# A new opening for a fused attention and feed-forward kernel: loads in the order k, q, v, the first block's attention in half blocks, and three PSUM banks shared by both layers

## The chip, the cores and the metric

The kernel runs on one core of a Trainium2 chip. The core has four compute engines that run side by side, each through its own list of instructions in order: TensorE (PE, matrix multiplication, with its weight loads shown apart as PEld), VectorE (DVE), ScalarE (ACT) and GpSimd (POOL). POOL also issues the loads of this kernel, SyncE (SP) the stores. The metric is the device time of one execution in microseconds; lower is better. Of the kernel before, three executions were timed: 582.8, 583.45 and 583.76 us, median 583.45.

## The reference

```python
def _attn_ref(q, k, v, E, F):            # q, k, v: 8 batches, 8 heads, 1024 tokens, 64 wide
    k_proj = np.einsum('ks,bhsd->bhkd', E, k)      # E, F: 64 x 1024
    v_proj = np.einsum('ks,bhsd->bhkd', F, v)
    scale = 1.0 / np.sqrt(q.shape[-1])
    scores = scale * np.matmul(q, k_proj.transpose(0, 1, 3, 2))
    scores = scores - np.max(scores, axis=-1, keepdims=True)
    attn = np.exp(scores)
    attn = attn / (np.sum(attn, axis=-1, keepdims=True) + 1e-09)
    return np.matmul(attn, v_proj)

def _moe_ref(x, w_in, w_out):            # x: 8192 x 512, w_in: 512 x 2048, w_out: 2048 x 512
    h = x @ w_in
    g = h * (1.0 / (1.0 + np.exp(-1.702 * h)))
    return (g @ w_out).astype(np.float32)
```

The attention output of all heads, 512 wide, is the x of the feed-forward layer. All inputs and the output are float32 in memory; the loads convert to bf16 on the way, and the multiplications take bf16 and add up in float32.

## The kernel before

**Tiling.** The 8 batches are cut into 16 blocks of 512 tokens, two to a batch. For a batch, TensorE projects k and v with E and F (`proj`, L112: eight matmuls for k and eight for v, which stand in alternation and write the two halves of one PSUM tile), transposes the projected k (L127) and q (`q_tr`, L141: four groups of eight transposes). For a block `h` and a pair of heads `p` there are one scores matmul with an exponential on ACT (`scores`, L155 and L158), and in `outp` one matmul with ones for the softmax's denominator (`d_ps`, L168), one for its numerator (`n_ps`, L170), a reciprocal on DVE (L172) and a product on DVE (L173) that gives a quarter of `xT`, the block's input to the feed-forward layer.

**Feed-forward layer.** `ffn1(j, fc)`, sixteen times a block: four matmuls of 128 x 512 (L184), then the gelu on ACT (L186). `ffn2(j, n, half)`, eight times a block: eight matmuls (L197), and after each second one a copy of the finished 128 x 512 output tile on ACT (L200). The exponential and the gelu need different tables on ACT; a table is loaded by ACT_TABLE_LOAD.

**Order.** It is written out by hand. A block has 24 slots: 16 after the `ffn1` calls and 8 after the `ffn2` calls. The table `fill` holds what is put into a slot. With `j0` the first block of batch `b`, block `j0 - 2` takes the projection of `b` (two of the eight steps in each of the slots 1 to 4), its output in slot 5, the q transposes in slots 8, 10, 12 and 14; the scores of block `h` stand in block `h - 2`, slots 16, 18, 20 and 22, and its `outp` in block `h - 1`, slots 0, 6, 12 and 17. Batch 0 and the scores of blocks 0 and 1 come before all that, with the four `outp` of block 0.

**PSUM.** Eight banks: two for `h_ps`, two for `o_ps`, two for everything named `s_ps`, one each for `d_ps` and `n_ps`.

**Loads.** All on POOL's queue, in this order: E, F, then of batch 0 k and v in halves by heads (k, v, k, v), q in eight pieces (one for each j, runs of 64 elements), w_in in four pieces, w_out in four, then k, v and q of batch 1. POOL issues at most eight that have not landed: the ninth waits for the first.

Of the kernel before, what the change touches and what calls it, by code (L numbers as in the profile page):

```python
# [17 lines left out]
def kernel(ctx, tc, q, k, v, E, F,  # L18
                                                     moe_w_in, moe_w_out, out):
    nc = tc.nc  # L20
# [46 lines left out]
    def load_kv(b, parts=1):  # L67
        kt[b] = ldpool.tile([P, H, J, D], BF16, name="k_sb")
        vt[b] = ldpool.tile([P, H, J, D], BF16, name="v_sb")
        hs = H // parts  # L70
        for i in range(parts):
            for src, dst in ((k, kt[b]), (v, vt[b])):
                nc.gpsimd.dma_start(  # L73
                    out=dst[:, i * hs:(i + 1) * hs],
                    in_=src[b, i * hs:(i + 1) * hs].rearrange("h (p j) d -> p h j d", p=P))
# [6 lines left out]

    nc.gpsimd.dma_start(out=ef_sb[:, 0, :], in_=E)
# [23 lines left out]
    def proj(b, j):  # L107
        def go():
            if j == 0:
                kvps[b] = ps_s.tile([P, H, D], F32, name="s_ps")  # L110
            for e, src in ((0, kt[b]), (1, vt[b])):
                nc.tensor.matmul(kvps[b][e * KP:(e + 1) * KP], eft[:, e, j, :], src[:, :, j, :],  # L112
                                 start=(j == 0), stop=(j == J - 1))
        return go

    def proj_out(b):
        def go():
            ps = kvps.pop(b)
            k_b = att.tile([KP, H, D], BF16, name="k_b")
            nc.vector.tensor_copy(k_b, ps[:KP])  # L120
            vv = ps[KP:].rearrange("k (p t) d -> k p t d", t=2)
            vbd = vbds[b % 2]
            nc.vector.tensor_copy(vbd[:KP, :, :D], vv[:, :, 0, :])
            nc.vector.tensor_copy(vbd[KP:, :, D:], vv[:, :, 1, :])  # L124
# [8 lines left out]

    def q_tr(b, g):
        def go():
            if g == 0:
                qT[b] = att.tile([P, HP, J, P], BF16, name="qT")
            t_ps = ps_s.tile([P, 2, HP, P], BF16, name="s_ps")
            for jj in range(2):
                for p in range(HP):  # L140
                    nc.tensor.transpose(  # L141
                        t_ps[:, jj, p, :],
                        qt[b][:, 2 * g + jj, 2 * p:2 * p + 2, :].rearrange("s t d -> s (t d)"), ident)
            nc.vector.tensor_copy(qT[b][:, :, 2 * g:2 * g + 2, :],  # L144
                                  t_ps.rearrange("r j p s -> r p j s"))
        return go
# [14 lines left out]
    def outp(h, p):  # L161
        b, c = divmod(h, S // TB)

        def go():
            if p == 0:
                xT[h] = att.tile([P, KC, TB], BF16, name="xT", bufs=3)
            d_ps = ps_n.tile([P, TB], F32, name="d_ps")
            nc.tensor.matmul(d_ps, ones2, expT[h][:, p, :], start=True, stop=True)  # L168
            n_ps = ps_n.tile([P, TB], F32, name="n_ps")
            nc.tensor.matmul(n_ps, vbds[b % 2][:, p, :], expT[h][:, p, :], start=True, stop=True)  # L170
            rden = att.tile([P, TB], F32, name="rden")
            nc.vector.reciprocal(rden, d_ps)  # L172
            nc.vector.tensor_tensor(xT[h][:, p, :], n_ps, rden, op=ALU.mult)  # L173
# [3 lines left out]
    gts, osb = {}, {}  # L177

    def ffn1(j, fc):
        if fc == 0:  # L180
            gts[j] = work.tile([P, FC, TB], BF16, name="gT")
        h_ps = ps_h.tile([P, TB], F32, name="h_ps")
        for kc in range(KC):
            nc.tensor.matmul(h_ps, w_in_sb[:, kc, fc * P:(fc + 1) * P], xT[j][:, kc, :],  # L184
                             start=(kc == 0), stop=(kc == KC - 1))
        nc.scalar.activation(gts[j][:, fc, :], h_ps, AF.Gelu_apprx_sigmoid)  # L186

    o_ps = {}

    def ffn2(j, n, half):  # L190
# [3 lines left out]
        if half == 0:  # L194
            o_ps[0] = ps_o.tile([P, DM], F32, name="o_ps")
# [13 lines left out]
    def at(j, slot, f):  # L209
        fill.setdefault((j, slot), []).append(f)  # L210

    NB2 = S // TB
    for b in range(1, B):
# [9 lines left out]
    for h in range(1, NBLK):  # L223
        for p, slot in enumerate((0, 6, 12, 17)):
            at(h - 1, slot, outp(h, p))


    for j in range(J):
        proj(0, j)()
    proj_out(0)()  # L230
    for g in range(J // 2):
        q_tr(0, g)()
    for h in range(NB2):
        for p in range(HP):
            scores(h, p)()
    for p in range(HP):
        outp(0, p)()
    load_kv(1)
    load_q(1)
# [43 lines left out]
```

## Time and profile before

| | |
|---|---|
| median of three executions | 583.45 us |
| profiled execution, its own time | 582.58 us |
| its span (first to last instruction) | 580.8 us |
| PE busy | 534.1 us, 92% of the span |
| DVE busy | 297.5 us, 51% |
| ACT busy | 264.9 us, 46% |
| POOL busy | 79.1 us, 14% |
| mean granted clock of TensorE | 0.978 |

The profile is one execution. The time of that execution is 1.78 us more than its span. "Granted clock" is the share of TensorE's full clock that it was given; a matmul on a granted clock of 0.50 takes twice as long to stream. A row of a timeline gives the start, the duration, the engine and line, the operation with output and input, and, in square brackets, how long the engine had been idle before it and which engine's or transfer's end released it. DMA traffic in GB/s counts the bytes as they are written, in bf16.

### The profile page before, as it was taken

How to read it: one execution, taken by the hardware profiler on the slowest of the kernel's cores; microseconds unless marked ns; L12 is line 12 of the kernel's file. 1: busy time of each engine (PE TensorE's matmuls, PEld its weight loads, DVE VectorE, ACT ScalarE, POOL GpSimd, SP SyncE). 2: the span in 40 equal slices, each digit the busy share in tenths (PEclk: the TensorE clock that was granted, in tenths of full speed). 3: DMA queues.
4: the chain of work that ended last, by engine and by line, in shares of the span. 5: the costliest groups of instructions: out<-in, count | busy, mean ns of one | idle time of the engine just before them, and what ended most of it. 6: DMA issues, size and time to landing. Idle time of an engine off the chain costs nothing.

```text
span 580.8 us, 6222 instructions
## 1 busy us (share of the span) xinstructions
PE 534.1 (92%) x2621; PEld 241.4 (42%) x2672; DVE 297.5 (51%) x209; ACT 264.9 (46%) x414; POOL 79.1 (14%) x98
## 2 busy tenths in 40 slices
PE   0635999999999999999999999999999999999997
PEld 0301444435444444435444444444444354444443
DVE  1385555547462764628373672737364573546200
ACT  0121446445463545545364545544464554645251
POOL 7533450013100140002300140000000000000000
PEclk9966999999999999999999999999999999999999
DMA  9999999029900691019910493010010101010001
GB/s 141 181 206 190 191 191 149 2 73 165 111 14 1 142 148 73 0 74 149 72 69 1 111 171 82 1 73 1 0 73 1 73 0 73 0 73 1 37 36 73
DMA packets 90379, 46.80 MB, mean 81 GB/s; under 512 B 67312, under 2 KB 87792, under 8 KB 88432
## 3 DMA queue, kind: packets, MB, share of 16 engines
q0 software_dynamic: 87616, 29.63, 45.7%
q1 hardware_dynamic: 2736, 16.78, 7.0%
q8 instruction: 21, 0.34, 0.2%
q14 instruction: 6, 0.05, 0.0%
HBM read 59.24 MB, written 16.78 MB: 131 GB/s over the span
## 4 chain that ended last, share of the span: by engine, by line
PE 85%; DMA 8%; ACT 5%; POOL 1%; issue 1%; ACTq 0%; POOLq 0%
PE o_ps L197 38%; PE h_ps L184 37%; DMA v_sb<-in_v_dram 6%; ACT L186 3%; PE s_ps L112 2%; PE s_ps L141 2%; PE s_ps L155 2%; PE n_ps L170 2%; DMA w_in_sb<-in_moe_w_in_dram 2%; PE d_ps L168 2%; ACT gT L186 1%; PE s_ps L127 0%; POOL k_sb L73 0%; ACT o_sb L200 0%; POOL q_sb L81 0%
## 5 line engine op out<-in xcount | busy, mean ns | idle before, releaser
L172 DVE RECIPROCAL rden<-d_ps 128x512 f32<-128x512 f32 x64 | 214.8, 3356 | 184.3 <-PE d_ps L168 179.7
L184 PE MATMUL h_ps<-xT,w_in_sb 128*128 128x512 bf16 x1000 | 243.9, 383 | 10.0 <-ACT gT L186 6.6
L197 PE MATMUL o_ps<-w_out_sb,gT 128*128 128x512 bf16 x1002 | 233.4, 379 | 1.2
L186 ACT ACTIVATE gT<-h_ps 128x512 bf16<-128x512 f32 x256 | 151.3, 597 | 131.8 <-PE h_ps L184 131.7
L184 PEld LDWEIGHTS <-w_in_sb 128*128 128x128 bf16 x1024 | 97.4, 98 | 130.7 <-issue 25.1
L197 PEld LDWEIGHTS <-gT 128*128 128x128 bf16 x1024 | 100.2, 98 | 120.8
L158 ACT ACTIVATE expT<-s_ps 128x512 bf16<-128x512 f32 x64 | 37.8, 597 | 88.1 <-PE s_ps L155 87.3
L200 ACT COPY o_sb<-o_ps 128x512 f32<-128x512 f32 x64 | 37.4, 585 | 86.0 <-PE o_ps L197 83.1
L81 POOL DMA_DIRECT2D q_sb<-in_q_dram x64 | 56.1, 902 | 79.9 <-PE s_ps L141 39.9
L173 DVE TENSOR_TENSOR xT<-n_ps,rden 128x512 bf16<-128x512 f32 x64 | 44.3, 692 | 6.7
L73 POOL DMA_DIRECT2D k_sb<-in_k_dram x9 | 7.7, 860 | 183.9 <-PE s_ps L112 181.3
L168 PE MATMUL d_ps<-expT,ones 128*128 128x512 bf16 x59 | 23.2, 394 | 8.6 <-DVE rden L172 8.6
L112 PE MATMUL s_ps<-k_sb,eft 128*64 128x512 bf16 x64 | 22.2, 437 | 9.0 <-DMA k_sb<-in_k_dram 9.0
L112 PE MATMUL s_ps<-v_sb,eft 128*64 128x512 bf16 x64 | 22.0, 440 | 5.7 <-DMA v_sb<-in_v_dram 5.7
L144 DVE COPY qT<-s_ps 128x1024 bf16<-128x1024 bf16 x32 | 21.3, 683 | 10.9 <-PE s_ps L141 10.9
L170 PE MATMUL n_ps<-expT,vbd 128*128 128x512 bf16 x64 | 25.1, 393 | 0.9 <-DVE xT L173 0.6
L155 PE MATMUL s_ps<-qT,kbd 128*128 128x512 bf16 x64 | 24.3, 380 | 1.4 <-ACT expT L158 0.8
L120 DVE CAST k_b<-s_ps 64x512 bf16<-64x512 f32 x8 | 5.5, 682 | 38.6 <-PE s_ps L112 38.6
L141 PE MATMUL s_ps<-ident,q_sb 128*128 128x128 bf16 x256 | 20.7, 230 | 0.6 <-DVE vbd L124 0.6
L141 PEld LDWEIGHTS <-q_sb 128*128 128x128 bf16 x256 | 18.2, 104 | 7.4 <-issue 0.7
L186 ACT ACT_TABLE_LOAD x15 | 19.2, 1283 | 4.2 <-PE h_ps L184 4.2
L158 ACT ACT_TABLE_LOAD x15 | 19.2, 1283 | 2.4 <-PE s_ps L155 1.4
(29 smaller groups left out, 60.4 us busy)
## 6 DMA issues: line engine op xcount, KB each, us to landing
out_dram<-o_sb SPq DMA_DIRECT2D x15, 1024.0 KB, 3.9
q_sb<-in_q_dram POOLq DMA_DIRECT2D x64, 128.0 KB, 6.0
k_sb<-in_k_dram POOLq DMA_DIRECT2D x7, 1024.0 KB, 10.5
v_sb<-in_v_dram POOLq DMA_DIRECT2D x7, 1024.0 KB, 14.6
w_in_sb<-in_moe_w_in_dram POOLq DMA_DIRECT2D x4, 512.0 KB, 10.7
w_out_sb<-in_moe_w_out_dram POOLq DMA_DIRECT2D x4, 512.0 KB, 17.5
k_sb<-in_k_dram POOLq DMA_DIRECT2D x2, 512.0 KB, 8.9
v_sb<-in_v_dram POOLq DMA_DIRECT2D x2, 512.0 KB, 10.6
```

The lines of the kernel that those rows point to most:

```text
L81: nc.gpsimd.dma_start(out=qt[b][:, j], in_=qv[:, j])
L112: nc.tensor.matmul(kvps[b][e * KP:(e + 1) * KP], eft[:, e, j, :], src[:, :, j, :], start=(j == 0), stop=(j == J - 1))
L141: nc.tensor.transpose(t_ps[:, jj, p, :], qt[b][:, 2 * g + jj, 2 * p:2 * p + 2, :].rearrange("s t d -> s (t d)"), ident)
L155: nc.tensor.matmul(s_ps, kbds[b % 2][:, p, :], qT[b][:, p, c * JB:(c + 1) * JB, :].rearrange("r j s -> r (j s)"), start=True, stop=True)
L158: nc.scalar.activation(expT[h][:, p, :], s_ps, AF.Exp, scale=scale)
L170: nc.tensor.matmul(n_ps, vbds[b % 2][:, p, :], expT[h][:, p, :], start=True, stop=True)
L172: nc.vector.reciprocal(rden, d_ps)
L173: nc.vector.tensor_tensor(xT[h][:, p, :], n_ps, rden, op=ALU.mult)
L184: nc.tensor.matmul(h_ps, w_in_sb[:, kc, fc * P:(fc + 1) * P], xT[j][:, kc, :], start=(kc == 0), stop=(kc == KC - 1))
L186: nc.scalar.activation(gts[j][:, fc, :], h_ps, AF.Gelu_apprx_sigmoid)
L197: nc.tensor.matmul(o_ps[0], gts[j][:, fc, n * P:(n + 1) * P], w_out_sb[:, fc, :], start=(fc == 0), stop=(fc == FC - 1))
L200: nc.scalar.copy(osb[j][:, n, :], o_ps[0])
```

## The change

**Loads.** k and q and v of batch 0 now come in this order, each in two pieces by j (runs of four j, 256 elements, that is 512 bytes as written), q no longer in eight pieces of 64-element runs but in the layout of k and v. Then w_in in eight pieces, w_out in four, and k, q, v of batch 1 right behind. Later batches load in the order k, q, v.

**Opening.** The k projection alone comes first, then the q transposes of block 0's half, the scores of block 0, and the denominators of its first 256 tokens (two pairs of heads to one PSUM tile of 128 x 512); then the second half of the q transposes, with their copies on ACT, the scores of block 1, a gelu table load, and only then the v projection, its casts on ACT, the numerators of the first 256 tokens and the denominators of the second. The transposes of batch 0 take one head at a time (64 of them in place of 32), because of q's new layout.

**Block 0.** Its `ffn1` runs as 16 calls on the first 256 tokens and 16 on the second, and the rest of the attention of blocks 0 and 1 and the work of batch 1 are put into its slots.

**Everywhere.** `h_ps` and `o_ps` share one pool of three banks, `d_ps` gets two and `n_ps` one; `outp` is cut into `den` and `num`; the projection goes in as two groups of four steps (slots 1 and 3); the scores stand in slots 16 to 19, followed by an explicit load of the gelu table in slot 20.

On ACT, in the opening, before (`expT` is the exponentials, `gT` the gelu outputs, each row with its count):

```order
L158 ACT_TABLE_LOAD
L158 ACTIVATE expT<-s_ps 128x512 x8
L186 ACT_TABLE_LOAD
L186 ACTIVATE gT<-h_ps 128x512 x16
L158 ACT_TABLE_LOAD
```

And in the changed kernel (`qT` the transposed q, `vbd` the projected v):

```order
L176 ACT_TABLE_LOAD
L176 ACTIVATE expT<-s_ps 128x512 x4
L163 COPY qT<-s_ps 128x4x256 x2
L176 ACTIVATE expT<-s_ps 128x512 x4
L180 ACT_TABLE_LOAD
L142 CAST vbd_91<-s_ps 64x4x64
L143 CAST vbd_91<-s_ps 64x4x64
L230 ACTIVATE gT<-h_ps 128x256 x32
L242 COPY o_sb<-o_ps 128x512 x4
```

Two qT copies and the two v casts moved to ACT; the gelu table load now stands ahead of the casts, and block 0 has 32 gelus of half the width.

On DVE, in the opening, before:

```order
L120 CAST k_b<-s_ps 64x512
L123 CAST vbd_91<-s_ps 64x4x64
L124 CAST vbd_91<-s_ps 64x4x64
L130 COPY kbd_90<-s_ps 64x4x64
L131 COPY kbd_90<-s_ps 64x4x64
L144 COPY qT<-s_ps 128x4x256 x4
L172 RECIPROCAL rden<-d_ps 128x512
L173 TENSOR_TENSOR xT<-n_ps,rden 128x512
```

And in the changed kernel:

```order
L127 CAST k_b<-s_ps 64x512
L133 COPY kbd_90<-s_ps 64x4x64
L134 COPY kbd_90<-s_ps 64x4x64
L163 COPY qT<-s_ps 128x4x256 x2
L204 RECIPROCAL rden<-d_ps 128x512 x2
L216 TENSOR_TENSOR xT<-n_ps,rden 128x2x256 x2
L204 RECIPROCAL rden<-d_ps 128x512 x2
L216 TENSOR_TENSOR xT<-n_ps,rden 128x2x256 x2
L204 RECIPROCAL rden<-d_ps 128x512 x2
L216 TENSOR_TENSOR xT<-n_ps,rden 128x512
L204 RECIPROCAL rden<-d_ps 128x512
L216 TENSOR_TENSOR xT<-n_ps,rden 128x512
```

Two reciprocals, not four with their products in between, stand ahead of the products on which block 0's first matmuls wait; behind them the reciprocals run ahead of the products by one or two.

On ACT, from one block's gelus to the next block's, in a later block, before:

```order
L186 ACTIVATE gT<-h_ps 128x512 x16
L158 ACT_TABLE_LOAD
L158 ACTIVATE expT<-s_ps 128x512
L200 COPY o_sb<-o_ps 128x512
L158 ACTIVATE expT<-s_ps 128x512
L200 COPY o_sb<-o_ps 128x512
L158 ACTIVATE expT<-s_ps 128x512
L200 COPY o_sb<-o_ps 128x512
L158 ACTIVATE expT<-s_ps 128x512
L200 COPY o_sb<-o_ps 128x512
L186 ACT_TABLE_LOAD
L186 ACTIVATE gT<-h_ps 128x512 x16
```

And in the changed kernel:

```order
L230 ACTIVATE gT<-h_ps 128x512 x16
L176 ACT_TABLE_LOAD
L176 ACTIVATE expT<-s_ps 128x512
L242 COPY o_sb<-o_ps 128x512
L176 ACTIVATE expT<-s_ps 128x512 x2
L242 COPY o_sb<-o_ps 128x512
L176 ACTIVATE expT<-s_ps 128x512
L180 ACT_TABLE_LOAD
L242 COPY o_sb<-o_ps 128x512 x2
L230 ACTIVATE gT<-h_ps 128x512 x16
```

The gelu table load moved from behind the block's last output copy to ahead of the last two; their number is the same.

```diff
-    ps_h = ctx.enter_context(tc.tile_pool(name="ps_h", bufs=2, space=PSUM))
-    ps_o = ctx.enter_context(tc.tile_pool(name="ps_o", bufs=2, space=PSUM))
+    ps_f = ctx.enter_context(tc.tile_pool(name="ps_f", bufs=3, space=PSUM))
     ps_s = ctx.enter_context(tc.tile_pool(name="ps_s", bufs=2, space=PSUM))
+    ps_d = ctx.enter_context(tc.tile_pool(name="ps_d", bufs=2, space=PSUM))
     ps_n = ctx.enter_context(tc.tile_pool(name="ps_n", bufs=1, space=PSUM))
...
+    def load_kv(src, dst, b, name, js=J):
+        dst[b] = ldpool.tile([P, H, J, D], BF16, name=name)
+        for j in range(0, J, js):
+            nc.gpsimd.dma_start(
+                out=dst[b][:, :, j:j + js],
+                in_=src[b].rearrange("h (p j) d -> p h j d", p=P)[:, :, j:j + js])
...
-    load_kv(0, parts=2)
-    load_q(0)
+    load_kv(k, kt, 0, "k_sb", JB)
+    load_kv(q, qt, 0, "q0_sb", JB)
+    load_kv(v, vt, 0, "v_sb", JB)
...
-    for i in range(4):
-        sl = slice(i * DFF // 4, (i + 1) * DFF // 4)
+    for i in range(8):
+        sl = slice(i * DFF // 8, (i + 1) * DFF // 8)
         nc.gpsimd.dma_start(out=w_in_sb[:, :, sl], in_=w_in_v[:, :, sl])
...
+    load(1)
...
+    def v_out(b):
+        def go():
+            vv = kvps.pop((b, 1))[KP:].rearrange("k (p t) d -> k p t d", t=2)
+            vbd = vbds[b % 2]
+            cp = nc.scalar.copy if b == 0 else nc.vector.tensor_copy
+            cp(vbd[:KP, :, :D], vv[:, :, 0, :])
+            cp(vbd[KP:, :, D:], vv[:, :, 1, :])
+        return go
...
+                if b == 0:
+                    for h in range(H):
+                        r = h % 2 * D
+                        nc.tensor.transpose(t_ps[r:r + D, jj, h // 2, :], qt[b][:, h, j, :], ident)
...
+            cp = nc.scalar.copy if b == 0 and g >= 2 else nc.vector.tensor_copy
+            cp(qT[b][:, :, 2 * g:2 * g + 2, :], t_ps.rearrange("r j p s -> r p j s"))
...
+    def gelu_table():
+        nc.scalar.preload_act_table(AF.Gelu_apprx_sigmoid)
+    def unit(h, p0, pn=1, half=None):
+        return (h, slice(p0, p0 + pn),
+                slice(0, TB) if half is None else slice(half * TB // 2, (half + 1) * TB // 2))
+    def over(ps, lhsT, u):
+        h, ps_, ts = u
+        for i, p in enumerate(range(ps_.start, ps_.stop)):
+            nc.tensor.matmul(ps[:, i, :], lhsT(p), expT[h][:, p, ts], start=True, stop=True)
+    def den(*a):
+        u = unit(*a)
+        def go():
+            d_ps = ps_d.tile(shape(u), F32, name="d_ps")
+            over(d_ps, lambda p: ones2, u)
+            rdens[a] = att.tile(shape(u), F32, name="rden", bufs=4)
+            nc.vector.reciprocal(rdens[a], d_ps)
+        return go
+    def num(*a):
...
+            n_ps = ps_n.tile(shape(u), F32, name="n_ps")
+            over(n_ps, lambda p: vbds[h // (S // TB) % 2][:, p, :], u)
+            nc.vector.tensor_tensor(xT[h][:, u[1], u[2]], n_ps, rdens.pop(a), op=ALU.mult)
+        return go
...
+    O = FC
+    proj(0, range(J), (0,))()
+    k_out(0)()
+    for g in (0, 1):
+        q_tr(0, g)()
+    for p in range(HP):
+        scores(0, p)()
+    den(0, 0, 2, 0)()
+    den(0, 2, 2, 0)()
+    for g in (2, 3):
+        q_tr(0, g)()
+    for p in range(HP):
+        scores(1, p)()
+    gelu_table()
+    proj(0, range(J), (1,))()
+    v_out(0)()
+    num(0, 0, 2, 0)()
+    num(0, 2, 2, 0)()
+    den(0, 0, 2, 1)()
+    den(0, 2, 2, 1)()
+    at(0, 9, num(0, 0, 2, 1))
+    at(0, 15, num(0, 2, 2, 1))
+    at(0, 16, den(1, 0), den(1, 1))
+    at(0, 23, num(1, 0))
+    at(0, 28, den(1, 2), num(1, 1))
+    at(0, 32 + 1, den(1, 3), num(1, 2))
+    at(0, 32 + 3, num(1, 3))
+    at(0, 32 + 5, proj(1, range(J), (0,)), k_out(1))
+    at(0, 32 + 6, q_tr(1, 0))
+    at(0, 32 + 7, q_tr(1, 1), *[scores(2, p) for p in range(HP)], gelu_table)
+    at(1, 2, q_tr(1, 2))
+    at(1, 4, q_tr(1, 3))
+    at(1, 5, proj(1, range(J), (1,)), v_out(1))
+    for p, slot in enumerate((6, 11, O, O + 2)):
+        at(1, slot, den(2, p), num(2, p))
...
-        for j in range(J):
-            at(j0 - 2, 1 + j // 2, proj(b, j))
-        at(j0 - 2, 5, proj_out(b))
+        for j in range(0, J, 4):
+            at(j0 - 2, 1 + j // 2, proj(b, range(j, j + 4)))
+        at(j0 - 2, 5, k_out(b), v_out(b))
...
-                at(j0 + c - 2, 16 + 2 * p, scores(j0 + c, p))
+                at(j0 + c - 2, O + p, scores(j0 + c, p))
+            at(j0 + c - 2, O + HP, gelu_table)
```

The slots of block 0 run to 39: 0 to 15 after the first half's `ffn1`, 16 to 31 after the second half's, 32 to 39 after the `ffn2` calls.

More of the change, by code (lines that the diff above doesn't have):

```diff
@@ L159, in scores @@
         return go
-    def outp(h, p):
-        b, c = divmod(h, S // TB)
-        def go():
-            if p == 0:
-                xT[h] = att.tile([P, KC, TB], BF16, name="xT", bufs=3)
[L167 to L173, printed above, removed]
-        return go
@@ L181, in ffn1 @@
+    gts, osb, o_ps = {}, {}, {}
+    def ffn1(j, fc, ts=slice(0, TB)):
+        if j not in gts:
             gts[j] = work.tile([P, FC, TB], BF16, name="gT")
-        h_ps = ps_h.tile([P, TB], F32, name="h_ps")
+        n = ts.stop - ts.start
+        h_ps = ps_f.tile([P, n], F32, name="h_ps", tag="f_ps")
         for kc in range(KC):
-            nc.tensor.matmul(h_ps, w_in_sb[:, kc, fc * P:(fc + 1) * P], xT[j][:, kc, :],
+            nc.tensor.matmul(h_ps, w_in_sb[:, kc, fc * P:(fc + 1) * P], xT[j][:, kc, ts],
@@ L185, in ffn1 @@
                              start=(kc == 0), stop=(kc == KC - 1))
-        nc.scalar.activation(gts[j][:, fc, :], h_ps, AF.Gelu_apprx_sigmoid)
-    o_ps = {}
+        nc.scalar.activation(gts[j][:, fc, ts], h_ps, AF.Gelu_apprx_sigmoid)
     def ffn2(j, n, half):
```

108 lines of the change are left out of this document (49 added, 59 removed).

## The prediction

> **What bounds the kernel now.** I read the page first (shares, groups), then the timeline of the opening, then TensorE's waits behind it.
>
> ```profile
> span 580.8 us, 6222 instructions
> PE 534.1 (92%) x2621; PEld 241.4 (42%) x2672; DVE 297.5 (51%) x209; ACT 264.9 (46%) x414; POOL 79.1 (14%) x98
> L172 DVE RECIPROCAL rden<-d_ps 128x512 f32<-128x512 f32 x64 | 214.8, 3356 | 184.3 <-PE d_ps L168 179.7
> L144 DVE COPY qT<-s_ps 128x1024 bf16<-128x1024 bf16 x32 | 21.3, 683 | 10.9 <-PE s_ps L141 10.9
> L200 ACT COPY o_sb<-o_ps 128x512 f32<-128x512 f32 x64 | 37.4, 585 | 86.0 <-PE o_ps L197 83.1
> L123 DVE CAST vbd<-s_ps 64x256 bf16<-64x256 f32 x8 | 3.4, 427 | 0.3
> ```
>
> TensorE bounds the kernel as a whole. Its idle time lies in the opening, in this timeline (start, duration, engine, line, operation; in brackets the idle time before and its releaser):
>
> ```profile
> 21.05 0.68 DVE L120 CAST k_b<-s_ps 64x512 bf16<-64x512 f32 x1 [14.71 <-PE s_ps L112]
> 21.80 0.39 PE L127 MATMUL s_ps<-ident,k_b 64*128 64x64 bf16 x4 [0.78 <-DVE k_b L120]
> 22.79 3.66 PE L141 MATMUL s_ps<-ident,q_sb 128*128 128x128 bf16 x32 [0.60 <-DVE vbd L124]
> 26.37 0.49 PE L155 MATMUL s_ps<-qT,kbd 128*128 128x512 bf16 x1
> 26.90 4.52 ACT L158 ACTIVATE expT<-s_ps 128x512 bf16<-128x512 f32 x8 [24.88 <-PE s_ps L155]
> 31.04 3.36 DVE L172 RECIPROCAL rden<-d_ps 128x512 f32<-128x512 f32 x1 [3.87 <-PE s_ps L155]
> 34.51 0.69 DVE L173 TENSOR_TENSOR xT<-n_ps,rden 128x512 bf16<-128x512 f32 x1
> 47.43 0.58 PE L184 MATMUL h_ps<-xT,w_in_sb 128*128 128x512 bf16 x1 [2.19 <-DVE xT L173]
> 54.67 0.59 PE L112 MATMUL s_ps<-v_sb,eft 128*64 128x512 bf16 x1 [3.76 <-DMA v_sb<-in_v_dram]
> ```
>
> Four reciprocals in series, each with its product, hold the first `ffn1` until 47.43; then the v of batch 1 stops TensorE until 54.67. From there it hardly stops. What is left are stops at block starts:
>
> ```profile
> PE h_ps L184 <- ACT gT L186: 6.6, 14, 0.7
> 90.35 0.58 ACT o_sb L200
> 90.95 1.28 ACT L186
> 92.24 0.61 ACT gT L186
> 92.24 1.09 ACT L186 ACTIVATE gT<-h_ps 128x512 bf16<-128x512 f32 x2
> 92.89 4.48 PE L184 MATMUL h_ps<-xT,w_in_sb 128*128 128x512 bf16 x20 [0.42 <-ACT gT L186]
> 97.20 0.38 PE L168 MATMUL d_ps<-expT,ones 128*128 128x512 bf16 x1
> 120.95 1.03 PE L184 MATMUL h_ps<-xT,w_in_sb 128*128 128x512 bf16 x4
> 159.19 4.48 PE L184 MATMUL h_ps<-xT,w_in_sb 128*128 128x512 bf16 x20 [0.73 <-ACT gT L186]
> 190.30 1.02 PE L184 MATMUL h_ps<-xT,w_in_sb 128*128 128x512 bf16 x4 [0.18 <-ACT gT L186]
> ```
>
> The last copy of a block is followed by the gelu table load, 1.28 us, and the third group of `ffn1` waits for a PSUM bank. Twenty matmuls from 92.89 to 97.20 give a step of 0.216 us. A matmul's row lasts 0.38, so a gap listed as 0.18 or 0.73 costs 0.16 more: 0.34 and 0.89.
>
> **Part 1: the loads.** The queue's own waits and the windows (width, PE, granted clock, DMA share, GB/s):
>
> ```profile
> 9.94 0.88 POOL L81 DMA_DIRECT2D q_sb<-in_q_dram  x1 [0.79 <-DMA k_sb<-in_k_dram]
> 12.49 0.87 POOL L81 DMA_DIRECT2D q_sb<-in_q_dram  x1 [1.67 <-DMA v_sb<-in_v_dram]
> 10.00:15.00 5.00, 0.07 (x1) 1.00 1.24 205
> 17.00:22.00 5.00, 3.80 (x19) 1.00 2.42 154
> 47.50:50.50 3.00, 3.00 (x7) 0.50 1.24 204
> 51.00:53.50 2.50, 0.00 (x0) 1.00 1.33 202
> 57.20:60.40 3.20, 3.20 (x11) 0.50 2.34 160
> 61.00:64.00 3.00, 3.00 (x19) 1.00 1.25 209
> ```
>
> The first piece of 512 KB is there at 9.9, the next 2.55 later. The new runs of 512 bytes as written lie between those of 1024 (205 GB/s) and q's of 128 (154). I take 200, nearer the first since a run of 512 has a quarter of the starts that q's has: 2.6 us a piece. Then k is complete at 12.5, q at 15.1 and 17.7, v at 20.3 and 22.9, w_in at 33.4, w_out at 43, k of batch 1 at 48. None of the last three is needed before it lands (below), so the load of batch 1 that stopped TensorE until 54.67 no longer does.
>
> **Part 2: the opening, on a half clock.** Second half of the k projection: 12.5 + 4 x 0.43 + 0.2 = 14.4 (0.43 is twice the step above). Cast 0.68 and transposes 0.4: 15.5. The first 32 one-head transposes cost 0.11 each if they run in series (3.66 / 32): 3.5 us; if two heads run side by side in the two column halves, as k and v do in the projection, 1.75. With the last qT copy of 0.68 behind, the scores of block 0 start between 18.2 and 19.9; I take 19. Four exponentials at 0.56 (4.52 / 8) and 0.53 ahead: 21.8. Denominators 0.85, then the second 32 transposes with their two copies on ACT, for which there is no row at 1024 elements: between 0.6 (512 take 0.585) and 1.2, taken 1.0. Scores of block 1 start at 25.4 to 27.0, taken 26.3; their exponentials end at 29.1. The v projection waits for an `s_ps` bank until 28.6 and takes 8 x 0.43 + 0.2: 32.2. The gelu table load, 29.1 to 30.4, is hidden below it, and costs its 1.3 if the projection gets shorter. Two casts on ACT, at most 0.585 each, taken 0.4: 33.1. Two times numerator (0.6) and product (0.69), one after the other since `n_ps` has one bank, with some 0.1 of handover: `ffn1` starts at **36.0**, bounds 34 and 38.5. The two reciprocals ahead, 21.9 to 28.6, are covered by the v chain.
>
> **Part 3: blocks 0 and 1.** TensorE's own work in block 0 at full clock: 128 half matmuls at 0.108 (bounds 0.108 and 0.12) 13.8; `ffn2` 64 x 0.216 = 13.8; numerators and denominators 4 x 0.108 + 8 x 0.216 = 2.2; k projection 1.9; transposes 1.1; scores 0.9. Sum 33.7. Stops: a half clock for 3.4 to 7 us more, worth 2.6 (bounds 1.7 and 3.5). The second half's last product stands one slot ahead of its first matmul: 0.75. In slot 28 the numerator waits for `n_ps`, whose product stands on DVE behind a second reciprocal (den(1,0), den(1,1), then the product: 2 x 3.36 + 0.7 after slot 16, where TensorE has 6.3 of work): 1.7, with the last three `ffn1` and all of `ffn2` queued behind it. The same in slot 35: 0.7. The k projection of batch 1 has its transposes straight behind the cast: 0.95. The scores of block 2 stand right behind the qT copy, 0.95, and share two banks with their exponentials, 1.35. Sum 9.0; block 1 starts at 36.0 + 33.7 + 9.0 = 78.7. Block 1: 27.6 + 0.9 + 1.9 + 1.7 + 0.9 = 33.0. Block 2 starts at 111.7, and not at 120.95: **9.3** gained. Both kernels have done the same work by then. w_out is used from 54, k of batch 1 from 65, v from 85; all have landed.
>
> **Part 4: blocks 2 to 14.** The gelu table now loads during `ffn2`, and a third bank lets `ffn1` run on. Even blocks lose 0.34 today, six times; odd ones and block 14 0.89, seven times: 8.3, all of it gained if nothing else comes last; none if ACT comes last all the same. The projection:
>
> ```profile
> 127.03 1.04 PE L184 MATMUL h_ps<-xT,w_in_sb 128*128 128x512 bf16 x4
> 127.99 0.40 PE L112 MATMUL s_ps<-k_sb,eft 128*64 128x512 bf16 x1
> 128.23 0.38 PE L112 MATMUL s_ps<-k_sb,eft 128*64 128x512 bf16 x1
> 128.55 1.04 PE L184 MATMUL h_ps<-xT,w_in_sb 128*128 128x512 bf16 x4
> ```
>
> Two steps take 0.56 and 0.1 of entry; two groups of four take 2 x (0.56 + 2 x 0.24 + 0.1) = 2.3 in place of 4 x 0.66 = 2.6; six times that is 2.2 gained (nothing, if the entry grows with the group). Scores in adjoining slots, `v_out` behind `k_out` and v loaded last cost nothing: an exponential of 0.6 fits below the 1.73 of a slot (eight matmuls), DVE is half idle, and a load has two blocks of time. **10.5** in all.
>
> **Sum.** 580.8 - 9.3 - 10.5 = 561.0 of span. The profiled execution took 582.58, 1.78 more than its span, and the median lies 0.87 above it: 561.0 + 1.78 + 0.87 = **563.7**.
>
> [...] By the chain above, copy, load (1.28) and gelu follow each other within 0.02 us. [...]
>
> **The rivals.**
> *The clock is full before `ffn1`.* After 3 us of unbroken work (47.5 to 50.5) the windows show a full clock, though TensorE then idles; 57.2 to 60.4 ends alike. The new opening is nearly unbroken from 20.2 to 25.5 if the transposes run in series. Then the v projection halves (1.7), numerators save 0.3 and the 2.6 of block 0 is gone: 563.7 - 4.6 = 559.1. Against it: the transposes from 22.79 still took 0.11 each, right after 3.5 us of projection, and 54.67 to 60.4 stayed at half. [...]
> *Half gelus bind.* If 256 elements cost ACT about as much as 512 (0.6; 0.5 back to back, by the two in the row from 92.24), 32 of them take 16 to 19 us against TensorE's 13.8: 4 more, 568.
> *The boundary gain fails.* The load moves, but ACT is still last with the first gelu: 8.3 lost, 572. Against it: after the early load only one copy of 0.585 stands ahead of that gelu.
> *Slower: short runs starve the weights.* k, q, v and w_in, 5.24 MB, now all come in runs of 512 bytes, and the first half block needs all of w_in. By the forecast that half is through at about 45 (36.0 and some 9 on the partly half clock); 20 us later, no gain is left. From 7.4 on that is a rate of 5240 / 57 = 92 GB/s; at 80 the end is 8 us beyond, near 592. Against it: 128-byte runs reached 154.
>
> **How the numbers follow.** Forecast 0.48, full clock early 0.30, half gelus 0.12, no boundary gain 0.07, starved 0.03. The forecast's own range, from the bounds of 36.0 and of the stops, is 561 to 567. The range given, 556.5 to 570, takes in the second and third case. A difference below 0.2% (1.2 us) could not be told from no change; faster 0.95, same 0.02, slower 0.03.
>
> **What would show it.** Right: `ffn1`'s first row near 36 with product and numerator just ahead; full clock some 5 us later; block 2 near 112; TensorE's waits for gT at later block starts gone; table loads ahead of the last two copies. Wrong: a clock of 1.00 already at 26; `ffn1` waiting for w_in; gT as the releaser all through block 0; a TensorE gap of more than 3 us at slots 28, 35 or 39, or a new wait in each block.

## The result, and the profile after

The changed kernel takes 557.09 us in the median (556.03 to 559.95), the one before 583.44 in the same series: a ratio of 0.9557, with a 95% interval of 0.9519 to 0.9596. The forecast was 563.7, in a range of 556.5 to 570. Three slow executions of the series below are left out of the medians and ratios: 1900.85 us of the kernel without the early table load (in its trace the matmuls of the two layers last 1011 and 1053 ns in the mean, 371 and 379 in the changed kernel, so this kernel was run a second time for a trace), 1702.99 of the reordered kernel, and 600.37 of the kernel before.

The page of the changed kernel, whose profiled execution (559.95 us) was the longest of its four:

```profile
span 558.2 us, 6473 instructions
PE 535.2 (96%) x2776; PEld 252.8 (45%) x2776; DVE 294.8 (53%) x205; ACT 269.0 (48%) x434; POOL 77.3 (14%) x96
L228 PE MATMUL h_ps<-xT,w_in_sb 128*128 128x512 bf16 (+1 forms) x1088 | 241.5, 371 | 0.7 <-DVE xT L216 0.6
```

TensorE is as busy as before (535 us), in a span that is 22.6 us shorter. Ahead of `ffn1` it was idle for 10.0 us in all before, 6.6 of them for gT; now for 0.7, and gT is no releaser.

The timeline of the opening and of blocks 0 and 1:

```profile
12.04 1.87 PE L119 MATMUL s_ps<-k_sb,eft 128*64 128x512 bf16 x4 [0.68 <-DMA k_sb<-in_k_dram]
15.00 1.92 PE L156 MATMUL s_ps<-ident,q_sb 128*64 128x128 bf16 x32
17.71 1.01 PE L173 MATMUL s_ps<-qT,kbd 128*128 128x512 bf16 x2 [0.79 <-DVE qT L163]
22.14 1.93 ACT L163 COPY qT<-s_ps 128x1024 bf16<-128x1024 bf16 x2 [1.46 <-PE s_ps L156]
24.12 0.59 PE L173 MATMUL s_ps<-qT,kbd 128*128 128x512 bf16 x2 [1.19 <-ACT qT L163]
26.24 3.53 PE L119 MATMUL s_ps<-v_sb,eft 128*64 128x512 bf16 x8 [0.20 <-ACT expT L176]
30.63 0.39 PE L192 MATMUL n_ps<-expT,vbd 128*128 128x256 bf16 x2 [0.85 <-ACT vbd L143]
32.45 6.49 PE L228 MATMUL h_ps<-xT,w_in_sb 128*128 128x256 bf16 x40
42.78 0.38 PE L228 MATMUL h_ps<-xT,w_in_sb 128*128 128x256 bf16 x2 [0.56 <-DVE xT L216]
50.58 0.38 PE L192 MATMUL n_ps<-expT,vbd 128*128 128x512 bf16 x1 [1.32 <-DVE xT L216]
59.92 0.38 PE L192 MATMUL n_ps<-expT,vbd 128*128 128x512 bf16 x1 [0.32 <-DVE xT L216]
66.38 0.29 PE L130 MATMUL s_ps<-ident,k_b 64*128 64x64 bf16 x4 [0.78 <-DVE k_b L127]
71.90 0.59 PE L173 MATMUL s_ps<-qT,kbd 128*128 128x512 bf16 x2 [0.78 <-DVE qT L163]
73.25 0.87 PE L173 MATMUL s_ps<-qT,kbd 128*128 128x512 bf16 x2 [0.76 <-ACT expT L176]
73.96 4.44 PE L228 MATMUL h_ps<-xT,w_in_sb 128*128 128x512 bf16 x12
108.79 1.03 PE L228 MATMUL h_ps<-xT,w_in_sb 128*128 128x512 bf16 x4
```

`ffn1` starts at 32.45 and hardly stops; the stops named in the prediction are there, each a little shorter. Block 1 starts at 73.96, block 2 at 108.79. Against 120.95 the opening and blocks 0 and 1 gave 12.2 us; from block 2 to the end it is 449.4 us now and was 459.9, so 10.4 more.

The windows of the same execution (stretch, width, PE busy, granted clock, DMA share, GB/s):

```profile
26.40:29.80 3.40, 3.37 (x8) 0.53 1.45 196
30.00:33.00 3.00, 1.46 (x11) 1.00 1.44 198
33.00:36.40 3.40, 3.40 (x17) 0.50 1.25 207
70.60:74.00 3.40, 1.74 (x14) 1.00 1.66 192
74.00:77.40 3.40, 3.40 (x10) 0.50 1.14 342
77.40:80.00 2.60, 2.60 (x20) 1.00 1.19 216
```

The clock does not rise once and stay. Up to 23 us TensorE is on half speed by the lengths of its rows (two scores matmuls take 1.01 at 17.71 and 0.59 at 24.12), although the windows there read 1.00: in this trace the record shows no half clock ahead of the first fall, and so the mean granted clock of an execution leaves this stretch out. Then the clock is full for the scores at 24, half for the v projection (3.53 us for eight matmuls, 1.91 in the k projection of batch 1 at 63.69), full again, half for the first 3.4 us of `ffn1`, and half once more for the first 3.4 us of block 1. Each of the three falls comes after a stretch in which TensorE was busy for about half of the time (1.48, 1.64 and 1.74 of the 3.4 us before).

### The profile page after: what moved, and what is told of

It reads as the page before. It is cut to its first block, busy times and chain, and to the rows that moved or that the text cites. A ratio compares the mean times of both kernels' runs of the same rounds, so it can differ in the third digit from the quotient of the medians.

```text
span 558.2 us, 6473 instructions
## 1 busy us (share of the span) xinstructions
PE 535.2 (96%) x2776; PEld 252.8 (45%) x2776; DVE 294.8 (53%) x205; ACT 269.0 (48%) x434; POOL 77.3 (14%) x96
## 4 chain that ended last, share of the span: by engine, by line
PE 93%; DVE 2%; ACT 2%; DMA 2%; issue 1%; POOL 0%; POOLq 0%
PE h_ps L228 40%; PE o_ps L239 39%; PE s_ps L119 4%; PE n_ps L192 3%; PE s_ps L173 2%; PE d_ps L192 2%; PE s_ps L159 2%; DMA k_sb<-in_k_dram 2%; DVE rden L204 1%; ACT expT L176 1%; DVE xT L216 1%; PE s_ps L156 1%; PE s_ps L130 0%; ACT qT L163 0%; DVE k_b L127 0%
## 5 line engine op out<-in xcount | busy, mean ns | idle before, releaser
L228 PE MATMUL h_ps<-xT,w_in_sb 128*128 128x512 bf16 (+1 forms) x1088 | 241.5, 371 | 0.7 <-DVE xT L216 0.6
L230 ACT ACTIVATE gT<-h_ps 128x512 bf16<-128x512 f32 (+1 forms) x272 | 155.5, 572 | 120.6 <-PE h_ps L228 119.4
L228 PEld LDWEIGHTS <-w_in_sb 128*128 128x128 bf16 x1088 | 105.3, 99 | 116.4 <-issue 10.6
L78 POOL DMA_DIRECT2D q_sb<-in_q_dram x56 | 49.0, 902 | 79.4 <-PE s_ps L159 59.4
L216 DVE TENSOR_TENSOR xT<-n_ps,rden 128x512 bf16<-128x512 f32 x64 | 44.0, 688 | 12.9 <-PE n_ps L192 7.0
L192 PE MATMUL n_ps<-expT,vbd 128*128 128x512 bf16 (+1 forms) x68 | 24.3, 366 | 3.3 <-DVE xT L216 2.4
L192 PE MATMUL d_ps<-expT,ones 128*128 128x512 bf16 (+1 forms) x68 | 24.4, 374 | 0.0
L119 PE MATMUL s_ps<-k_sb,eft 128*64 128x512 bf16 x64 | 18.3, 415 | 4.3 <-DMA k_sb<-in_k_dram 4.3
L119 PE MATMUL s_ps<-v_sb,eft 128*64 128x512 bf16 x64 | 18.1, 414 | 0.2 <-ACT expT L176 0.2
L159 PE MATMUL s_ps<-ident,q_sb 128*128 128x128 bf16 x224 | 17.1, 219 | 0.0
L119 PEld LDWEIGHTS <-eft 128*64 128x64 bf16 x128 | 8.5, 115 | 18.1 <-issue 14.4
```

The lines of the kernel that those rows point to most:

```text
L78: nc.gpsimd.dma_start(out=qt[b][:, j], in_=qv[:, j])
L119: nc.tensor.matmul(kvps[b, e][e * KP:(e + 1) * KP], eft[:, e, j, :], (kt, vt)[e][b][:, :, j, :], start=(j == 0), stop=(j == J - 1))
L159: nc.tensor.transpose(t_ps[:, jj, p, :], qt[b][:, j, 2 * p:2 * p + 2, :].rearrange("s t d -> s (t d)"), ident)
L192: nc.tensor.matmul(ps[:, i, :], lhsT(p), expT[h][:, p, ts], start=True, stop=True)
L216: nc.vector.tensor_tensor(xT[h][:, u[1], u[2]], n_ps, rdens.pop(a), op=ALU.mult)
L230: nc.scalar.activation(gts[j][:, fc, ts], h_ps, AF.Gelu_apprx_sigmoid)
```

## The experiments

### Which of two edits took the waits at the block starts away

The prediction gave 8.3 us to the early table load and the third bank together. Two kernels take one away or add one alone. First the changed kernel without the early load in blocks 1 to 13:

```diff
-    at(1, O + HP, gelu_table)
-            at(j0 + c - 2, O + HP, gelu_table)
```

> The changed kernel without the explicit gelu table load in blocks 1 to 13, so that the load falls due again at each block's first gelu; three shared banks stay. If the early load is what took the waits at the block starts away (part 4 of the prediction), they come back: 0.34 in even and 0.89 us in odd blocks and block 14, about 8 us in all, and the stretch from the start of block 2 to the end goes from 449.4 to about 457 us. Rival: the third bank alone covers the load. After a block's last matmul ACT needs copy 0.6, a wait of 0.3 for the first group, load 1.28 and gelu 0.6, 2.8 us, while TensorE has three groups of 0.86 and the 0.43 of a denominator and numerator, 3.0: then the stretch stays at 449 to 450 us and the time does not change.

Measured: 558.23 us, ratio to the kernel before 0.9557 (0.953 to 0.9584), the same as with the load. The same kernel, run again:

> The same kernel as the one without the early gelu table load, since the profile of the first was of an execution in which TensorE ran at less than a third of its speed throughout. If the third bank alone covers the load, TensorE shows no wait for gT at any block start and the stretch from block 2 to the end is 449 to 450 us; if not, 457.

Measured: 556.04 and 561.10 us, ratio 0.9603 (0.9561 to 0.9645). The timeline of the execution of 556.04, span 554.3 us: first TensorE's start of block 2, then ACT's table load and TensorE's third and fourth groups:

```profile
104.70 1.03 PE L228 MATMUL h_ps<-xT,w_in_sb 128*128 128x512 bf16 x4
105.81 1.28 ACT L230 ACT_TABLE_LOAD   x1 [0.32 <-PE h_ps L228]
107.94 1.90 PE L228 MATMUL h_ps<-xT,w_in_sb 128*128 128x512 bf16 x8
```

The table load is back where it was, and no row of TensorE from here on waits for gT. From 104.70 to the end it is 449.6 us. So in the changed kernel the early load is worth nothing: the third bank covers it.

Next the kernel before with the early load alone:

```diff
+    def gelu_table():
+        nc.scalar.preload_act_table(AF.Gelu_apprx_sigmoid)
...
+            at(j0 + c - 2, 16 + 2 * HP - 2, gelu_table)
```

> The kernel before, and in it only the early gelu table load, behind the last exponential of a block in slot 22, so ahead of the block's last output copy. PSUM pools as before (two banks for each layer). If the early load is enough by itself, TensorE's 6.6 us of listed waits for gT go (8.3 us from block 2 on) and the time falls from 583.4 to about 575; if it is the third bank that does it, the time stays within 1 us of 583.4.

And the kernel before with one pool of four banks for both layers, without the early load:

```diff
-    ps_h = ctx.enter_context(tc.tile_pool(name="ps_h", bufs=2, space=PSUM))
-    ps_o = ctx.enter_context(tc.tile_pool(name="ps_o", bufs=2, space=PSUM))
+    ps_f = ctx.enter_context(tc.tile_pool(name="ps_f", bufs=4, space=PSUM))
...
-        h_ps = ps_h.tile([P, TB], F32, name="h_ps")
+        h_ps = ps_f.tile([P, TB], F32, name="h_ps", tag="f_ps")
...
-            o_ps[0] = ps_o.tile([P, DM], F32, name="o_ps")
+            o_ps[0] = ps_f.tile([P, DM], F32, name="o_ps", tag="f_ps")
```

> The kernel before, and in it only one pool of four banks for both layers in place of two and two; no early table load. If a third bank for the first groups of a block covers the table load, the listed waits of 6.6 us go and the time falls to about 575; if the early load is needed, it stays within 1 us of 583.4.

Measured: 573.99 us with the early load, ratio 0.9833 (0.9805 to 0.9862), and 574.18 us with the four shared banks, ratio 0.9837 (0.9817 to 0.9858). ACT at the start of block 2, with the early load, where the load ends before the last copy:

```profile
119.06 1.28 ACT L178 ACT_TABLE_LOAD   x1
120.36 0.59 ACT L203 COPY o_sb<-o_ps 128x512 f32<-128x512 f32 x1
121.10 0.60 ACT L189 ACTIVATE gT<-h_ps 128x512 bf16<-128x512 f32 x1 [0.15 <-PE h_ps L187]
```

and with four shared banks, where it comes behind the copy as in the kernel before:

```profile
121.01 1.28 ACT L185 ACT_TABLE_LOAD   x1 [0.32 <-PE h_ps L183]
```

In neither does TensorE wait for gT at all. Each edit alone takes the waits away whole, 7.7 us (from block 2 on 452.2 us in both, against 459.9), and in the changed kernel the second of them adds nothing. The expectation of the first run of this part, that the waits come back without the early load, was wrong, and its rival right; here each edit turned out to be enough, so neither is the cause against the other.

### The projection in groups of four

```diff
-        for j in range(0, J, 4):
-            at(j0 - 2, 1 + j // 2, proj(b, range(j, j + 4)))
+        for j in range(0, J, 2):
+            at(j0 - 2, 1 + j // 2, proj(b, range(j, j + 2)))
```

> The changed kernel with the projection of batches 2 to 7 again in four groups of two steps (slots 1 to 4). By part 4 each group has an entry and an exit worth about 0.2 us, so the stretch from the start of block 2 to the end gets 2.2 us longer (0.36 in each of six blocks), 451.6. Rival: the cost goes with the steps, not the groups; then it stays at 449.4. The time itself moves by no more than its scatter between executions.

Measured: 559.52 us, ratio 0.9585 (0.9564 to 0.9605). Its page:

```profile
span 557.7 us, 6473 instructions
```

and in its timeline the scores of block 2, the start of block 1 and that of block 2:

```profile
70.44 0.59 PE L173 MATMUL s_ps<-qT,kbd 128*128 128x512 bf16 x2 [0.78 <-DVE qT L163]
71.79 0.86 PE L173 MATMUL s_ps<-qT,kbd 128*128 128x512 bf16 x2 [0.76 <-ACT expT L176]
72.49 2.75 PE L228 MATMUL h_ps<-xT,w_in_sb 128*128 128x512 bf16 x12
105.64 1.03 PE L228 MATMUL h_ps<-xT,w_in_sb 128*128 128x512 bf16 x4
```

452.1 us from block 2 on, 2.65 more than the changed kernel (2.2 expected). The cost goes with the groups. Together with the 7.7 of the runs above that makes the 10.4. The first rows matter below, for the clock: up to block 2 this kernel is the changed one, the two stops are the same 0.78 and 0.76, and yet block 1 starts here on a full clock (2.75 for twelve matmuls, and not 4.44).

### The loads

v ahead of q:

```diff
-    load_kv(q, qt, 0, "q0_sb", JB)
     load_kv(v, vt, 0, "v_sb", JB)
+    load_kv(q, qt, 0, "q0_sb", JB)
```

> The changed kernel with v of batch 0 loaded ahead of q (k, v, q), everything else the same. If the order of the loads sets the opening, q's first piece lands at about 20 and not 15 us, the scores of block 0 begin at 22.5 to 23 in place of 17.7, and the first ffn1 starts about 5 us later, near 37.5; the time is 4 to 6 us longer. Rival: TensorE and ACT set the opening, and v's landing at 23 leaves slack for q; then the first ffn1 starts within 1 us of 32.5.

Measured: 561.99 us, ratio 0.9665 (0.963 to 0.9699). Its timeline:

```profile
20.78 1.92 PE L156 MATMUL s_ps<-ident,q_sb 128*64 128x128 bf16 x32 [4.93 <-DMA q_sb<-in_q_dram]
37.96 4.82 PE L228 MATMUL h_ps<-xT,w_in_sb 128*128 128x256 bf16 x40
```

TensorE stands for 4.9 us until q is there, and `ffn1` starts 5.5 us later, 4.7 of it counted from k's second half, which landed 0.8 later in this execution. The order k, q, v is worth some 5 us (4.9 by the medians, 6 by the ratios).

q in short runs again, with two-head transposes:

```diff
-    load_kv(q, qt, 0, "q0_sb", JB)
+    load_q(0)
-                if b == 0:
+                if b < 0:
```

> The changed kernel with q of batch 0 in eight pieces of 64-element runs, as before, and so 32 transposes of two heads in place of 64 of one head. If the long runs matter, q at 154 GB/s lands 0.8 (first four pieces) and 1.6 us (all) later and v and the weights 1.6 later; the first ffn1 starts 1 to 2 us later. Rival: q is waited for by nobody after TensorE has done the k projection at 15.0 us, and the start stays within 0.5 us of 32.5. The transposes: if one-head transposes run side by side, 32 of them take as long as 16 of two heads, and this form takes about the same 1.9 us a half.

Measured: 557.28 us, ratio 0.9581 (0.9549 to 0.9614).

```profile
12.92 1.86 PE L119 MATMUL s_ps<-k_sb,eft 128*64 128x512 bf16 x4 [1.05 <-DMA k_sb<-in_k_dram]
15.89 1.89 PE L159 MATMUL s_ps<-ident,q_sb 128*128 128x128 bf16 x16
33.19 6.48 PE L228 MATMUL h_ps<-xT,w_in_sb 128*128 128x256 bf16 x40
```

k landed 0.9 later in this execution; counted from k's second half, `ffn1` starts after 20.3 us here and after 20.4 in the changed kernel. Nobody waits for q in either. The long runs are worth nothing that can be measured, and the 32 one-head transposes they bring take 1.92 us, as long as 16 of two heads. So two run side by side. It is not that a matmul with half as many columns of weights is shorter: in the k projection of batch 1, on a full clock, eight matmuls of 128*64 take 1.91 us, as eight of 128*128 do in `ffn1` (1.89).

### The half blocks

```diff
-    den(0, 0, 2, 0)()
-    den(0, 2, 2, 0)()
+    den(0, 0)()
+    den(0, 1)()
...
+    den(0, 2)()
     proj(0, range(J), (1,))()
     v_out(0)()
-    num(0, 0, 2, 0)()
-    num(0, 2, 2, 0)()
-    den(0, 0, 2, 1)()
-    den(0, 2, 2, 1)()
+    den(0, 3)()
+    for p in range(HP):
+        num(0, p)()
...
+    for p, slot in enumerate((0, 6, 12, O + 1)):
+        at(0, slot, den(1, p), num(1, p))
...
-        halves = 2 if j == 0 else 1
+        halves = 1
```

> The changed kernel without the half blocks: four denominators of 512 tokens each, two ahead of the second half of the q transposes, one ahead of and one behind the v projection, then the four numerators; block 0 runs its ffn1 on 512 tokens, and the attention of block 1 is in slots 0, 6, 12 and 17 as in the other blocks. Four reciprocals then stand ahead of the products, two more at 3.36 each, though about 4 us of them fall below the v chain (27.1 to 31.1). If the half blocks are worth what is left, the fourth product comes near 37.5 to 38.5 and not at 32.9, and the time is 3 to 6 us longer, less the waits in block 0 that go with the halves (1.3, 0.6 and 0.3 us). Rival: those waits and the clock weigh as much, and the time is the same within 2 us.

Measured: 561.39 us, ratio 0.9637 (0.9611 to 0.9662).

```profile
34.99 0.59 PE L192 MATMUL n_ps<-expT,vbd 128*128 128x512 bf16 x1 [3.86 <-DVE xT L216]
38.11 1.91 PE L228 MATMUL h_ps<-xT,w_in_sb 128*128 128x512 bf16 x4
76.61 4.44 PE L228 MATMUL h_ps<-xT,w_in_sb 128*128 128x512 bf16 x12
```

The second numerator waits 3.9 us for the first product, which stands behind four reciprocals, and `ffn1` starts 5.7 later, of which 0.9 is k, that landed later in this execution. Counted from k's second half it is 4.8 at `ffn1` and 1.8 at the start of block 1 (76.61 against 73.96): the rest comes back in block 0, where the half blocks have their own stops. In the ratios they are worth 0.8%, some 4 to 5 us. That is not theirs alone: the slots of block 1's attention moved with them, and the granted clock was lower in these executions (0.985 to 0.994).

### The clock

The changed kernel with idle multiplications in TensorE's gaps, some of which are shown; more stand in the other gaps up to `ffn1` and at the end of block 0. They change no result.

```diff
+    def warm(n):
+        def go():
+            w_ps = ps_f.tile([P, TB], F32, name="w_ps", tag="f_ps")
+            for _ in range(n):
+                nc.tensor.matmul(w_ps, ones2, eft[:, 0].rearrange("p j k -> p (j k)"),
+                                 start=True, stop=True)
+        return go
...
-    proj(0, range(J), (0,))()
+    warm(7)()
+    proj(0, range(JB), (0,))()
+    warm(2)()
+    proj(0, range(JB, J), (0,))()
```

> The changed kernel with idle multiplications on TensorE (a constant tile against the transposed E, into a bank that nobody reads) in the gaps of the opening and of the end of block 0: seven ahead of the first k piece, two to four in each gap up to the first ffn1, three behind the k projection of batch 1 and three twice around the scores of block 2. If the half clock is what stretches the opening and what makes the executions differ by 4 us, the granted clock is full from about 13 us on, the v projection takes 1.8 in place of 3.5, the cold stretches at 33 to 36.4 and 74 to 77.4 go (1.7 each), and the time falls to 552 to 554 with a smaller scatter. Rival: the clock costs little, since TensorE waits for ACT and DVE in the opening anyway; then the time stays at 556 to 558.

Measured: 553.97 us (553.43 to 554.11), ratio 0.951 (0.9492 to 0.9527). The mean granted clock is 0.999 to 1.0 in all four executions; in those of the changed kernel it was 0.991 to 0.999, and the one at 0.991 was the longest. Four rows of its timeline, the transposes of block 0, the v projection and the starts of `ffn1` and block 1:

```profile
15.07 1.08 PE L166 MATMUL s_ps<-ident,q_sb 128*64 128x128 bf16 x32 [0.61 <-DMA q_sb<-in_q_dram]
24.68 1.89 PE L127 MATMUL s_ps<-v_sb,eft 128*64 128x512 bf16 x8 [0.20 <-ACT expT L186]
29.24 4.82 PE L238 MATMUL h_ps<-xT,w_in_sb 128*128 128x256 bf16 x40
69.11 2.75 PE L238 MATMUL h_ps<-xT,w_in_sb 128*128 128x512 bf16 x12
```

and the window ahead of block 1:

```profile
64.00:68.00 4.00, 3.87 (x26) 1.00 2.16 164
```

The transposes take 1.1 and not 1.9, the v projection 1.9 and not 3.5, the first forty half matmuls 4.8 and not 6.5, and the first twelve of block 1 2.75 and not 4.44. The half clock cost about 3 us in the median and 6.6 in the profiled execution (by the spans, 558.2 and 551.6).

The scatter shrinks too, from 3.9 us to 0.7 in four executions each. That the clock makes all of it is not shown, and the mean granted clock does not put the executions in order: without the early load one took 556.04 at 0.990 and another 561.10 at 0.991, and in the first run of that kernel, of 557.11, 557.69 and 558.76, the longest was the one at 1.0. Where the half clock falls differs between them. On the page of the execution at 0.990 the clock stands at 0.6 in the slice from 13.9 to 27.7 us, in which TensorE is busy for 0.7 of the time, and at 0.9 or more in every other, and block 1 starts on a full clock (2.75 us for its first twelve matmuls, from 71.55); in the changed kernel's trace 3.4 us of it fall on the v projection, 3.4 on `ffn1` and 3.4 on block 1. The landing of k's second half moves as well, from 12.0 to 12.9 us in these traces.

### The stops in block 0

The changed kernel with other slots in block 0, so that each product stands on DVE ahead of the next reciprocal, and the work of batch 1 has an `ffn2` group between a cast or copy and its reader:

```diff
-    at(0, 16, den(1, 0), den(1, 1))
-    at(0, 23, num(1, 0))
-    at(0, 28, den(1, 2), num(1, 1))
-    at(0, 32 + 1, den(1, 3), num(1, 2))
-    at(0, 32 + 3, num(1, 3))
-    at(0, 32 + 5, proj(1, range(J), (0,)), k_out(1))
-    at(0, 32 + 6, q_tr(1, 0))
-    at(0, 32 + 7, q_tr(1, 1), *[scores(2, p) for p in range(HP)], gelu_table)
+    at(0, 16, den(1, 0))
+    at(0, 20, num(1, 0), den(1, 1))
+    at(0, 28, num(1, 1), den(1, 2))
+    at(0, 32 + 1, num(1, 2), den(1, 3))
+    at(0, 32 + 3, num(1, 3), proj(1, range(J), (0,)))
+    at(0, 32 + 4, k_out(1), q_tr(1, 0))
+    at(0, 32 + 5, q_tr(1, 1))
+    at(0, 32 + 6, scores(2, 0), scores(2, 1))
+    at(0, 32 + 7, scores(2, 2), scores(2, 3), gelu_table)
```

> The changed kernel with other slots in block 0 only: of block 1, denominator 0 in slot 16, numerator 0 and denominator 1 in slot 20, numerator 1 and denominator 2 in slot 28, numerator 2 and denominator 3 in slot 33, numerator 3 in slot 35, so that each product stands on DVE ahead of the next reciprocal; of batch 1, the k projection in slot 35, its output and the first q transposes in slot 36, the second in slot 37, the scores of block 2 in slots 38 and 39. No work is added or left out. If the stops that part 3 counted are real costs, those at n_ps (1.3 and 0.3 us listed), behind the k projection (0.8) and around the scores of block 2 (0.8 and 0.8) go, 4 to 4.5 us, and so does the cold stretch at 74 to 77.4 that follows the last two: 552 to 553.5. Rival: DVE's chain of eight reciprocals sets block 0's length whatever the order; then it stays at 556 to 557.

Measured: 552.88 us, ratio 0.9494 (0.9476 to 0.9513).

```profile
31.64 4.82 PE L228 MATMUL h_ps<-xT,w_in_sb 128*128 128x256 bf16 x40
66.67 2.75 PE L228 MATMUL h_ps<-xT,w_in_sb 128*128 128x512 bf16 x12
100.08 1.03 PE L228 MATMUL h_ps<-xT,w_in_sb 128*128 128x512 bf16 x4
```

From the first `ffn1` to block 1 it is 35.0 us, 41.5 before the edit; 1.7 of the difference is the clock at the first forty matmuls, the remaining 4.8 the stops. The trace without the early load has the old slots and, on its page, a clock of 0.9 or more in this stretch: 39.9, so 4.8 again. Block 1 takes 33.4 and not 34.8, since its start is no longer on a half clock. The stops were real, and DVE's eight reciprocals are no bound.

### Both together

The fillers of the opening (not those at the end of block 0), the slots above, and, as a third edit, the v projection moved between the second and third scores of block 1:

```diff
-    for p in range(HP):
-        scores(1, p)()
-    gelu_table()
+    warm(4)()
+    scores(1, 0)()
+    scores(1, 1)()
     proj(0, range(J), (1,))()
     v_out(0)()
+    scores(1, 2)()
+    warm(3)()
+    scores(1, 3)()
+    gelu_table()
```

> The idle multiplications of the opening (not those at the end of block 0) and the slots of the reordered kernel together; also the v projection between the second and third scores of block 1, so that its casts on ACT come ahead of the last two exponentials. If clock and stops are separate costs, the gains add: 554.0 less about 1.6 (n_ps), 2.9 (end of block 0, where the fillers took 3 us that are now work) and 1.2 (opening), 548 to 549. Rival: the clock and the stops are one cost (a stop matters through the clock it loses); then it comes out at 552 to 554.

Measured: 548.71 us (547.66 to 548.79), ratio 0.9429 (0.9417 to 0.9442): 5.7% below the kernel before, and 1.3% below the changed one by the ratios.

```profile
29.05 4.82 PE L238 MATMUL h_ps<-xT,w_in_sb 128*128 128x256 bf16 x40
64.08 2.75 PE L238 MATMUL h_ps<-xT,w_in_sb 128*128 128x512 bf16 x12
97.49 1.03 PE L238 MATMUL h_ps<-xT,w_in_sb 128*128 128x512 bf16 x4
```

It beats both: 35.0 us from `ffn1` to block 1 as in the reordered kernel, and the start of `ffn1` as in the filled one. By the ratios the fillers alone gave 0.5% and the slots alone 0.6%, so the gains add in full. The little that is left over cannot be told from the third edit, which has no run of its own: counted from k's second half, `ffn1` starts 0.9 earlier than in the filled kernel.

## Why the prediction was right, and where it missed

**The direction was right, and so was most of the mechanism: the gains came where the four parts put them.** The forecast of 563.7 is 6.6 above the measured median. The forecast's own range of 561 to 567 does not hold the median; the range that was given does, by 0.6 at its lower end, because it was widened for two rivals, neither of which came about as described. So that it held is in part luck. The error has three parts. The sum for a profiled execution was 561.0 + 1.78 = 562.8, and the profiled one took 559.95: 2.8 too much. In the forecast the opening was 3.5 too long and block 0 1.2 too long, while block 1 was 1.8 too short, so that misses cancel. The 0.87 that I added, since the median before lay above its profile, had the wrong sign: the profiled execution was the longest of four, 2.86 above the median. The two make up the other 3.7.

**Part 1, the loads.** Right: 196 to 198 GB/s while the 512-byte runs move, 200 taken. It put no price on q's place ahead of v, which is worth some 5 us by the run with v ahead of q; that q's longer runs matter was not claimed, and they do not.

**Part 2, the opening, is the step that failed:** 36.0 against 32.45. The transposes were taken half way between serial and side by side; they run side by side, and that brought the scores of block 0 forward by 0.8 and those of block 1 by 0.9 more. Another 0.5 came from the k projection, which ended at 13.9 and not 14.4, and 0.3 from the v projection and its casts. The last 1.0 lies behind the casts. About half of it is the clock: two numerators took 0.39, and not the 0.6 of a half clock. The other half was a plain error in the chain: the first `ffn1` needs the first product for its first two matmuls and waits for the second product only in the middle (32.45, with the second product done at 32.9), while I let it start after both products and the handover. The two copies on ACT (0.97 each, 1.0 taken) and the casts (0.37 each, 0.4 taken) were right.

**The clock was neither the forecast's nor the first rival's.** I had it half up to `ffn1` and some us beyond, and then full; the rival had it full from about 25 on. In the profiled execution it went up, down, up, down, up, and down again at block 1. The forecast had 2.6 for `ffn1` (1.7 measured) and nothing for block 1 (1.7). The 2.6 stood for 3.4 to 7 us on half clock, for which the prediction shows no row; in the trace before the clock reads 0.50 from 54 to 60 us, and from the start of `ffn1` it was 3.4 us. In the changed kernel's trace a half-busy stretch cost its stops and, at `ffn1` and at block 1, half of the next 3.4 us on top (1.7); but the clock did not fall after every such stretch. In the trace with groups of two TensorE's rows in the 3.4 us ahead of block 1 are those of the changed kernel, with the same stops of 0.78 and 0.76, and the clock stayed full (2.75 us for twelve matmuls, 4.44 in the changed kernel). What decides between the two, no run shows. The first rival's time, 559.1, is nearer to the median than the forecast, and inside the scatter of the executions; its mechanism, one early rise, is not what the trace shows.

**Part 3, blocks 0 and 1.** The stops came where they were named: 0.56, 1.32, 0.32, 0.78, 0.78 and 0.76 listed, with 0.16 more for each, 5.5 in all against 6.4 forecast for them. Block 0 took 41.5 (42.7 forecast), block 1 34.8 (33.0 forecast, the difference being the clock: without the early load and with groups of two block 1 starts on a full clock and takes 33.15).

**Part 4, blocks 2 to 14.** 10.5 forecast, 10.4 measured. The size was right, the reason half right: I gave the 8.3 to the early load and the third bank as if both were needed. Either is enough, and it is worth 7.7. The groups of the projection gave 2.65, not 2.2. The two misses cancel.

**The other rivals.** Half gelus do not bind: in block 0 they are released by TensorE's matmuls, and 256 elements take 0.38 us. The boundary gain did not fail. The short runs starved nothing. A table load cost its 1.28 us and nothing on top: in the rows of the run with the early load alone the copy follows the load within 0.02 us (load until 120.34, copy at 120.36), and with four shared banks so does the gelu (load until 122.29, gelu at 122.31).

## What to carry to other kernels

A wait that two edits can remove is worth its price once; try each alone before paying for both. In a stage whose limit is a chain through three engines, write the chain down to the first instruction that needs its end, since half a result may be enough to start. And look at the clock behind a gap as well as at the gap: here, where TensorE was busy for 1.48 to 1.74 of 3.4 us, the next 3.4 us ran at 0.50 in one trace, and behind the same stops at full clock in another. Idle multiplications in the gaps took 3.1 us off the median; useful work moved into them took 4.8 us off the way from `ffn1` to block 1, beside the clock.

## What the runs showed of the hardware that I had not expected

The granted clock fell to 0.50 after stretches in which TensorE was busy for 1.48, 1.64 and 1.74 of 3.4 us, and stayed there for 3.4 us each time; in the trace with groups of two it stayed full behind the same rows ahead of block 1 (twelve matmuls in 2.75 us). How far a rule can be made of that, three falls in one trace do not show. Multiplications that nobody reads kept it at 1.00 in every window from 6 to 38 us and from 64 to 72, and took about 3 us off the median (557.09 to 553.97). The recorded clock can read 1.00 where TensorE is slow: from 15 to 17 us it does, while 32 transposes take 1.92 us that take 1.08 with the fillers. Two transposes of 128 x 64 into different column halves run side by side: on half speed 32 take 1.92 us, where 16 of 128 x 128 take 1.89.
